# Batch 2's x turned by transfers, two expert units halved, and batch 3's q and k turned half a block sooner

## The chip, the cores and the metric

The kernel runs on one core of a Trainium2 chip. The metric is the device time of one execution in microseconds (us); less is better. The core's engines run side by side, each through its own list of instructions in order, and wait for one another by semaphores: TensorE (PE: matmuls, with weight loads, PEld, beside them), VectorE (DVE), ScalarE (ACT), GpSimd (POOL) and SyncE (SP), which here only issues transfers. A transfer (DMA) is issued by an engine's queue and carried out by the core's 16 DMA engines.

## The reference

Two layers follow each other. The first is attention over 8 batches, 8 heads, 576 positions and head size 64, with a sliding window of 128 and a bias linear in the distance. The second takes its result as 4608 tokens of 512 values through 8 dense experts, whose weights per token come from a table that is normalised by rows and columns in turn, eight times.

```
scores = scale * q @ k.T + bias, masked to 0 <= rel < 128
x      = softmax(scores) @ v                   # reshaped to 4608 x 512
P      = exp(x @ w_gate - max)
8 times: P /= P.sum(1);  P /= P.sum(0);  P *= N / E
out    = sum over e of P[:, e] * (relu(x @ w1[e]) @ w2[e])
```

## The kernel before

**Numbering.** Batches count from 0, so the "third batch" is batch 2 and the "fourth" batch 3. A batch has four blocks of 128 positions and a tail of 64; x block `blk` of batch b is 4b + kb, and the tails of two batches share one of the blocks 32 to 35.

**Stages.** The first stage (to about 250 us) does the attention and, woven between, experts 0 and 1, which don't need the table P. Then the table is normalised, with what is left of experts 0 and 1 filling TensorE. From about 325 us to the end, experts 2 to 7 are done for 18 groups of two blocks in a form of Strassen's product.

**Attention steps.** The loop over `steps` (line 695 on) goes through batch b, key block kb and half of the heads u; `at` = 2 kb + u counts the ten steps of a batch. For the step after, it issues the scores (`psS`, TensorE, line 438), their exponentials (`pt`, ScalarE, line 444) and the mask multiplication (VectorE, line 449). For the step itself it issues the values (`psN`, TensorE, line 472), then on VectorE a reciprocal (line 482) and the normalised x (`xsb`, line 483). The scores of batch b start at the last step of batch b - 1.

**Turning q and k.** q and k are loaded as float32 on SyncE's queue (`load_qk`), cast to `c16` by `cast_qk` (q on VectorE line 298, k on GpSimd line 296 where `pool` is set), and, from batch XPE = 3 on, turned by two transposing transfers on SyncE's queue (`turn_qk`, line 313). `order_qk` (line 324) then copies them into `kN` (GpSimd) and `qN` (VectorE). In batch b, the casts for batch b + 1 stand at steps 8 and 9 of b - 1 and 0 and 1 of b, the transfers and the four `kN` copies at step 1 and the `qN` copies, in pairs, at steps 6 and 7. For batch 3 all four casts stand at steps 0 and 1 of batch 2. Batches 0 to 2 are turned by TensorE.

**Turning x.** Expert matmuls need x with features on partitions (`xT`). `by_pe` says which batches are turned by TensorE: four transposes into `psX` (line 511) and a copy by VectorE (line 522), issued at the next step. The others are turned by one transposing transfer on SyncE's queue per block (line 524). `keep_x` (line 499) also stores each block to DRAM (`xd`) three blocks later, on SyncE's or GpSimd's queue.

**Expert units.** A unit is (expert, first block, number of blocks). Its first layer is eight atoms: four matmuls into `psh` (line 117) and a relu by ScalarE into `hT` (line 129). Its second layer is one atom per block: eight matmuls into `psy` (line 141), then a cast to `yo` by VectorE (line 560) and a store to `ysp` by SyncE (line 546). `hT` has two buffers. `psh`, `psy`, `psN`, `psX` and `psG` (the gates, line 532) share the four banks of the pool tag `pmm` in turn, so each has to wait until the one four places before it has been read.

**Order.** The order is written out at build time, since the program records under a manual schedule. `order` (line 563) lists the units; `Filler` takes the first whose blocks are all below `filler.ready` and deals out its atoms between the attention instructions: per step `filler.fill(1.0)` ahead of the values and the rest of `budget` behind them. `budget` is the backlog of ready units, by the planner's 0.87 us for a first-layer atom of four blocks (`L1_US`) and 1.74 us for a second-layer atom (`L2_US`), divided by the steps left. In batches 0 to 2 `ready` grows block by block; from batch 3 on, at step 0 of each later batch, to all blocks of the batches before.

Of the kernel before, what the change touches and what calls it, by code (L numbers as in the profile page):

```python
# [14 lines left out]
def kernel(  # L15
# [10 lines left out]
    nc = tc.nc  # L26
# [4 lines left out]
    B, H, S, Dh = q.shape  # L31
# [11 lines left out]
    RI = 4  # L43
# [127 lines left out]
    XPE, YO, XSB = 3, 7, 12  # L171
# [61 lines left out]
    if True:  # L233
# [34 lines left out]
        def load_tail(b):  # L268
            t32 = asb.tile([P, H, Dh], FP32, name=f"t32_{b}", tag="s32", bufs=5)
            for lo, src in ((0, q), (TL, k)):  # L270
                nc.sync.dma_start(
                    out=t32[lo : lo + TL], in_=src[b, :, SM:S, :].rearrange("h s d -> s h d")
                )
            tails[b] = t32
# [13 lines left out]
        def cast_qk(b, j, which=(1, 0), pool=False):  # L288

            if b not in c16s:  # L290
                c16s[b] = per.tile([P, 2, RI, H, Dh], FP16, name=f"c16_{b}", tag="a8", bufs=8)
            for n in which:
                src = raw[b][n][:, 2 * j : 2 * j + 2, :].rearrange("p h (i d) -> p i h d", i=RI)
                to = c16s[b][:, n, :, 2 * j : 2 * j + 2, :]
                if pool:
                    nc.gpsimd.tensor_copy(out=to, in_=src)
                elif n == 0:
                    nc.vector.tensor_copy(out=to, in_=src)
                else:
                    nc.scalar.copy(out=to, in_=src)  # L300
# [8 lines left out]
        def turn_qk(b):  # L309
            c16 = c16s.pop(b)  # L310
            qk = per.tile([P, 2, RI, NDT, P], FP16, name=f"qk_{b}", tag="a8", bufs=8)
            for n in range(2):
                nc.sync.dma_start(
                    out=qk[:, n].rearrange("p i j r -> p (i j) r"),
                    in_=c16[:, n].rearrange("p i h d -> p (i h d)"),
                    transpose=True,
                )
            KT[b] = qk
            homes(b)

        def order_qk(b, n, js):

            for j in js:
                (nc.vector, nc.gpsimd)[n].tensor_copy(
                    out=QKT[b][n][:, j].rearrange("p (r i) -> p r i", i=RI),
                    in_=KT[b][:, n, :, j, :].rearrange("p i r -> p r i"),
                )
# [3 lines left out]
        def cast_tail(b):  # L331
            t16s[b] = asb.tile([P, HD], FP16, name=f"t16_{b}", tag="t16", bufs=1)
            nc.gpsimd.tensor_copy(out=t16s[b], in_=tails.pop(b).rearrange("p h d -> p (h d)"))
# [154 lines left out]
            )  # L488

        def by_pe(b):  # L490
            return b < XPE or b == B - 1

        kept: list = []

        def keep_x(left=0):
            while len(kept) > left:
                blk, lo, nk, xsb = kept.pop(0)
                queue = nc.gpsimd if 2 * RI <= blk < 6 * RI else nc.sync
                queue.dma_start(out=xd[blk, lo : lo + nk, :], in_=xsb[0:nk].rearrange("p h d -> p (h d)"))

        def turn_x(b, kb):
            nk = sizes(kb)
            blk = 4 * b + kb if kb < NKB - 1 else 4 * B + b // 2
            lo = 0 if kb < NKB - 1 else TL * (b % 2)
            xT, at = x_of(blk)
            to = xT[:, at, :, lo : lo + nk]
            xsb = xsbs.pop((b, kb))
            if by_pe(b):
                ps = aps.tile([P, NDT, P], FP16, name=f"psX_{b}_{kb}", tag="pmm", bufs=4)
                for j in range(NDT):  # L510
                    nc.tensor.matmul(
                        out=ps[:, j, 0:nk],
                        lhsT=xsb[0:nk, 2 * j : 2 * j + 2, :],
                        rhs=ident[0:nk, 0:nk],
                        is_transpose=True,
                        start=(j == 0),
                        stop=(j == NDT - 1),
                    )
                if b == 0:
                    nc.scalar.copy(out=to, in_=ps[:, :, 0:nk])  # L520
                else:
                    nc.vector.tensor_copy(out=to, in_=ps[:, :, 0:nk])
            else:
                nc.sync.dma_start(out=to, in_=xsb[0:nk].rearrange("p h d -> p (h d)"), transpose=True)
            kept.append((blk, lo, nk, xsb))
            keep_x(3)
# [16 lines left out]
        def store(left=0):  # L543
            while len(stores) > left:
                e, blk, yo = stores.pop(0)
                nc.sync.dma_start(out=ysp[e, blk], in_=yo)
# [15 lines left out]

        order = [(0, 0, 2), (0, 2, 2)]
        for b0 in range(RI, NBLK, 4):
            order += [(0, b0, 4), (1, b0 - 4, 4)]
        order.append((1, NBLK - 4, 4))
        filler = Filler(
            (*unit, lambda unit=unit: unit_atoms(*unit, aps, ("pmm", "pmm"), (4, 4), keep))
# [126 lines left out]
        for n, (b, kb, u) in enumerate(steps):  # L695
            nxt = steps[n + 1] if n + 1 < len(steps) else None
            at = 2 * kb + u
# [44 lines left out]
            if n > 0 and u == 0 and by_pe(steps[n - 1][0]):  # L742
                turn_x(*steps[n - 1][:2])
# [11 lines left out]
            if u == 1 and not by_pe(b):  # L755
                turn_x(b, kb)
# [23 lines left out]
                cast_qk(b + 2, at - 8, (1,), True)  # L780
                cast_qk(b + 2, at - 8, (0,))
            if XPE <= b + 1 < B:
                if at == 0 and b + 1 == XPE:
                    for j in range(2):
                        cast_qk(b + 1, j, (1,), True)
                        cast_qk(b + 1, j, (0,))
                if at < 2:
                    cast_qk(b + 1, at + 2, (1,), True)
                    cast_qk(b + 1, at + 2, (0,))
                if at == 1:  # L790
                    store(1)
                    turn_qk(b + 1)
                    order_qk(b + 1, 1, range(NDT))
                if at == 5:
                    cast_tail(b + 1)
                if at in (6, 7):
                    order_qk(b + 1, 0, range(2 * at - 12, 2 * at - 10))
            if b < B - 1 and at == (1 if b > 1 else 5) and b:
                load_tail(b + 1)
            if 10 * b + at >= 66:  # L800
# [21 lines left out]
        filler.fill(1.0)  # L822
        turn_x(B - 1, NKB - 1)
        keep_x()
        filler.fill(2.6)
        gates(4 * B - 4, NBLK)
# [432 lines left out]
```

## Time and profile before

| | |
|---|---|
| median of 3 runs | 1003.75 us (1002.99 to 1004.34) |
| the profiled execution | 1004.55 us, its span 1002.8 us |
| TensorE busy | 990.0 us, 99% of the span |
| VectorE, ScalarE, GpSimd busy | 762.8, 717.6, 111.0 us |
| batch 2, from its scores to batch 3's | 71.08 to 101.47 us |
| batch 3, from its scores to batch 4's | 101.47 to 133.02 us |
| DMA engines | 122.46 MB, 122 GB/s on average |

A profile row names line, engine, operation and `out<-in`; an `x16` counts instructions, and `idle` or a bracket gives the engine's pause before them and what ended it. A timeline row gives the start and the length of instructions of one kind that follow each other. Matmuls are pipelined, so their lengths overlap; the distance of two starts is the cost. Buffer numbers are left out of names, so `psh` is any first-layer tile; in the text `psh_10_4` is atom 4 of the unit that starts at block 10, and "(b, kb, u)" is an attention step.

### The profile page before, as it was taken

To read this page: it belongs to the slowest core of one execution; us is meant where nothing else is said; L and a number is where in the kernel's file an instruction comes from. 1 tells how busy PE (TensorE), PEld (TensorE's weight loads), DVE (VectorE), ACT (ScalarE), POOL (GpSimd) and SP (SyncE) were. 2 spreads that over 40 slices of the span, in tenths; PEclk is the share of its full clock that TensorE was granted. 3 is DMA by queue.
4 is the path that set the end of the run, shared out by engine and by line. 5 is a ranking of instruction groups with operands and counts; after the bars stand their busy time and mean duration, and the time that the engine had idled before them with its cause. 6 is when DMAs were issued, how large, how long until landed. Compare 5 with 4: busy or idle time off the path is not lost.

```text
span 1002.8 us, 27976 instructions
## 1 busy us (share of the span) xinstructions
PE 990.0 (99%) x11591; PEld 801.7 (80%) x11591; DVE 762.8 (76%) x1598; ACT 717.6 (72%) x1216; POOL 111.0 (11%) x198
## 2 busy tenths in 40 slices
PE   7999999999999999999999999999999999999998
PEld 5655544455544899999999999999999999999997
DVE  6746677666688989887887887787787787787777
ACT  7655554555334768888888888888888888888875
POOL 3314345355010000000000000000000000000000
PEclk9999999999999999999999999999999999999999
DMA  9998799999997324334333333434433333333361
GB/s 244 220 261 212 169 231 227 214 188 172 235 194 167 75 54 97 82 61 99 81 63 93 86 72 79 86 71 79 96 76 64 98 78 66 96 78 67 92 117 48
DMA packets 262895, 122.46 MB, mean 122 GB/s; under 512 B 201968, under 2 KB 253680, under 8 KB 262768
## 3 DMA queue, kind: packets, MB, share of 16 engines
q1 hardware_dynamic: 247264, 100.58, 45.2%
q0 software_dynamic: 15072, 19.93, 11.4%
q8 instruction: 90, 1.47, 0.6%
q14 instruction: 37, 0.30, 0.1%
q10 hardware_dynamic: 432, 0.16, 0.1%
HBM read 78.30 MB, written 23.59 MB: 102 GB/s over the span
## 4 chain that ended last, share of the span: by engine, by line
PE 93%; DVE 3%; DMA 2%; ACT 2%; issue 0%; DVEq 0%; ACTq 0%
PE psM L1030 31%; PE psB L993 14%; PE psh L117 12%; PE psy L141 12%; PE psA L993 9%; PE psC L993 9%; PE psS L438 1%; PE psN L472 1%; DMA k<-in_k_dram 1%; DVE pt L449 1%; ACT pt L444 1%; PE psh L972 1%; DMA xset<-xs 1%; PE psT L368 0%; DVE xsb L483 0%
## 5 line engine op out<-in xcount | busy, mean ns | idle before, releaser
L1030 PEld LDWEIGHTS <-hs 128*128 128x128 f16 x2996 | 271.0, 98 | 22.4 <-DVE hs L1010 0.4
L1030 PE MATMUL psM<-w2l,hs 128*128 128x256 f16 x1440 | 186.6, 273 | 0.2 <-DVE hs L1010 0.2
L993 PEld LDWEIGHTS <-w1l 128*128 128x128 f16 x2848 | 181.4, 98 | 4.8 <-issue 0.2
L1006 ACT ACTIVATE hs<-hs 128x512 f16<-128x512 f16 x212 | 130.3, 629 | 35.7 <-DVE hs L1176 26.1
L1176 DVE TENSOR_TENSOR hs<-psB,s5y 128x512 f16<-128x512 f32 x106 | 73.2, 691 | 98.7 <-ACT xs L902 93.3
L993 PEld LDWEIGHTS <-s 128*128 128x128 f16 x2136 | 141.7, 98 | 7.1 <-issue 0.6
L129 ACT ACTIVATE hT<-psh 128x512 f16<-128x512 f32 (+1 forms) x144 | 84.0, 586 | 76.9 <-PE psh L117 76.9
L117 PE MATMUL psh<-xT,w1t 128*128 128x512 f16 (+1 forms) x608 | 137.5, 368 | 1.1 <-DMA xT<-xsb 1.1
L902 ACT ACTIVATE xs<-xtok,L_sb 128x512 f16<-128x512 f16 x204 | 135.8, 720 | 2.5 <-DMA xset<-xs 2.4
L141 PE MATMUL psy<-w2t,hT 128*128 128x512 f16 x576 | 135.2, 379 | 0.0
L1030 PE MATMUL psM<-more,hs 128*128 128x256 f16 x864 | 129.4, 273 | 0.0
L993 PE MATMUL psB<-xset,s 128*128 128x128 f16 x1424 | 108.5, 219 | 0.5 <-ACT psB L1155 0.5
L993 PE MATMUL psA<-xset,w1l 128*128 128x128 f16 x1424 | 108.5, 219 | 0.0
L444 ACT ACTIVATE pt<-psS 128x1024 f16<-128x1024 f32 x64 | 64.5, 1021 | 58.3 <-PE psS L438 57.4
L141 PEld LDWEIGHTS <-hT 128*128 128x128 f16 x576 | 53.6, 98 | 59.4 <-issue 1.9
L117 PEld LDWEIGHTS <-w1t 128*128 128x128 f16 x608 | 55.2, 98 | 53.8 <-issue 3.9
L1010 DVE TENSOR_TENSOR hs<-hs 128x1024 f16<-128x1024 f16 x107 | 73.8, 690 | 20.4 <-ACT hs L1006 18.3
L1167 ACT COPY psC<-psB 128x512 f32<-128x512 f32 x106 | 60.4, 570 | 38.4 <-PE psB L993 38.4
L449 DVE TENSOR_TENSOR pt<-pt,mask 128x1024 f16<-128x1024 f16 x64 | 52.3, 818 | 38.7 <-ACT pt L444 38.7
L560 DVE CAST yo<-psy 128x512 f16<-128x512 f32 x65 | 44.6, 690 | 44.4 <-PE psy L141 42.0
L1159 ACT COPY s5y<-psC 128x512 f32<-128x512 f32 x106 | 62.2, 587 | 22.4 <-PE psC L993 22.4
L595 POOL DMA_DIRECT2D w2t<-in_moe_w_dram x2 | 1.8, 886 | 668.8 <-DVE xset L926 660.8
(128 smaller groups left out, 1497.2 us busy)
## 6 DMA issues: line engine op xcount, KB each, us to landing
s5y<-ysp SPq DMA_DIRECT2D x36, 256.0 KB, 3.0
ysp<-yo SPq DMA_DIRECT2D x65, 128.0 KB, 4.2
v<-in_v_dram SPq DMA_DIRECT2D x32, 256.0 KB, 5.0
out_dram<-acc SPq DMA_DIRECT2D x31, 256.0 KB, 2.5
q<-in_q_dram SPq DMA_DIRECT2D x5, 1024.0 KB, 7.9
k<-in_k_dram SPq DMA_DIRECT2D x5, 1024.0 KB, 9.0
xtok<-xd SPq DMA_DIRECT2D x34, 128.0 KB, 2.3
w2t<-in_moe_w_dram POOLq DMA_DIRECT2D x4, 1024.0 KB, 12.1
```

Source lines behind the costliest of these rows:

```text
L117: nc.tensor.matmul(out=ps[:, 0:nt], lhsT=w1ts[e][:, dt, P * ft : P * ft + P], rhs=xT[:, at : at + nb, dt, :], start=(dt == 0), stop=(dt == ...
L129: nc.scalar.activation(out=st["hT"][:, ft, 0:nt], in_=ps[:, 0:nt], func=AF.Relu)
L141: nc.tensor.matmul(out=ps, lhsT=st["hT"][:, ft, P * ms : P * ms + P], rhs=w2ts[e][:, ft, :], start=(ft == 0), stop=(ft == NFT - 1),)
L444: nc.scalar.activation(out=pt, in_=ps.rearrange("p a y n -> p (a y) n"), func=AF.Exp, scale=scale)
L449: nc.vector.tensor_tensor(out=pt, in0=pt, in1=mask_of[kb][:, 4 * u : 4 * u + 4, :], op=ALU.mult)
L902: nc.scalar.mul(out=xs[2 * (n % 2) + m], in_=xtok[m], mul=P_sb[:, blk, e : e + 1])
L993: nc.tensor.matmul(out=ps[:, j, :], lhsT=q[k][:, P * j : P * j + P], rhs=xset[n % 2][:, x, P * k : P * k + P], start=(start and j == 0 and ...
L1006: nc.scalar.activation(out=h[n][:, slot], in_=src, func=AF.Relu)
L1010: nc.vector.tensor_tensor(out=t[:, 4:6], in0=t[:, 0:2], in1=t[:, 2:4], op=ALU.add)
L1030: nc.tensor.matmul(out=Ms[bk][:, half, :], lhsT=h[n][:, LEFT[m], f, :], rhs=W2L[e][RIGHT[m]][:, f, :], start=(e == 2 and f == 0 and half = ...
L1159: nc.scalar.copy(out=s5, in_=pc)
L1176: nc.vector.tensor_tensor(out=h[n][:, 3], in0=pb, in1=s5, op=ALU.add)
```

## The change

Three things are changed together.

- `by_pe` leaves out batch 2: its five x blocks are turned by transfers on SyncE's queue, at the second half of their own step. The `xd` stores of batch 1's four full blocks move to GpSimd's queue.
- The units (0,8,4) and (0,12,4) of expert 0 become (0,8,2), (0,10,2) and (0,12,2), (0,14,2). A half unit's first layer has eight atoms of matmuls 256 wide.
- For batch 3, casts 0 and 1 move from step 0 of batch 2 to step 9 of batch 1, casts 2 and 3 to step 0, and `turn_qk` and the `kN` copies from step 1 to step 0.

Because half a unit is ready sooner, expert 0's first half on batch 2 now runs in batch 2's own steps instead of batch 3's. From batch 5 on TensorE's order is the same.

```diff
         def by_pe(b):
-            return b < XPE or b == B - 1
+            return b < XPE - 1 or b == B - 1
...
-                queue = nc.gpsimd if 2 * RI <= blk < 6 * RI else nc.sync
+                queue = nc.gpsimd if RI <= blk < 6 * RI else nc.sync
...
         for b0 in range(RI, NBLK, 4):
-            order += [(0, b0, 4), (1, b0 - 4, 4)]
+            order += [(0, b0, 2), (0, b0 + 2, 2)] if b0 in (4 * XPE - 4, 4 * XPE) else [(0, b0, 4)]
+            order.append((1, b0 - 4, 4))
...
             if XPE <= b + 1 < B:
-                if at == 0 and b + 1 == XPE:
-                    for j in range(2):
-                        cast_qk(b + 1, j, (1,), True)
-                        cast_qk(b + 1, j, (0,))
-                if at < 2:
-                    cast_qk(b + 1, at + 2, (1,), True)
-                    cast_qk(b + 1, at + 2, (0,))
-                if at == 1:
+                first = b + 1 == XPE
+                for j in ((2, 3) if first else (at + 2,)) if at < 2 - first else ():
+                    cast_qk(b + 1, j, (1,), True)
+                    cast_qk(b + 1, j, (0,))
+                if at == 1 - first:
                     store(1)
                     turn_qk(b + 1)
                     order_qk(b + 1, 1, range(NDT))
...
+            if (b, at) == (XPE - 2, 9):
+                for j in range(2):
+                    cast_qk(XPE, j, (1,), True)
+                    cast_qk(XPE, j, (0,))
```

## The prediction

> **What bounds the kernel now.** I read the page's busy times and its chain first, then the timeline of each engine around the batches that the change touches.
>
> ```profile
> PE 990.0 (99%) x11591; PEld 801.7 (80%) x11591; DVE 762.8 (76%) x1598; ACT 717.6 (72%) x1216; POOL 111.0 (11%) x198
> PE 93%; DVE 3%; DMA 2%; ACT 2%; issue 0%; DVEq 0%; ACTq 0%
> L117 PE MATMUL psh<-xT,w1t 128*128 128x512 f16 (+1 forms) x608 | 137.5, 368 | 1.1 <-DMA xT<-xsb 1.1
> ```
>
> TensorE is busy 99% of the span and carries 93% of the chain. From 50 to 325 us it hardly pauses, and after batch 4 both programs give it the same matmuls in the same order. So the time moves by the TensorE work that is removed or added in batches 2 to 4, and by TensorE pauses that go or come there. The only pause that the group lines charge to a transfer in this stage is the 1.1 us for `xT`.
>
> ```profile
> 25.87 3.66 PE L117 MATMUL psh<-xT,w1t 128*128 128x256 f16 x32
> ...
> 95.02 0.41 PE L472 MATMUL psN<-v,pt 128*128 128x65 f16 x8
> 95.26 0.39 PE L511 MATMUL psX<-ident,xsb 128*128 128x128 f16 x4
> 95.48 3.62 PE L141 MATMUL psy<-w2t,hT 128*128 128x512 f16 x16
> ...
> 137.49 0.61 PE L438 MATMUL psS<-qN,kN 64*128 64x256 f16 x8
> 139.22 1.02 PE L117 MATMUL psh<-xT,w1t 128*128 128x512 f16 x4 [1.12 <-DMA xT<-xsb]
> ```
>
> In this TensorE timeline (start, length) the reader is to see the starts: lengths overlap by a drain, so costs are taken from start to start. A turn of x by TensorE (`psX`) costs 0.22 us here (95.26 to 95.48). Matmuls 256 wide come every 0.109 us ((3.66 - 0.27) / 31); those 512 wide every 0.216.
>
> **The change, part by part.** The sum is made against the profiled execution (1004.55 us, span 1002.80) and then taken off the median 1003.75, which is 0.80 lower.
>
> 1. *Batch 2 by transfers.* Twenty transposes leave TensorE: five groups of 0.39 (83.71 to 84.10), 0.22, 0.22, 0.22 and 0.31: -1.36 us. The fourth really spans 0.32, but 0.10 of that is the lead-in of the scores behind it, which stays (132.68 to 133.02 against 95.02 to 95.26); the fifth adds 0.09 to the values ahead of it. VectorE loses four `xT` copies of 0.41 and one of 0.28; it was not what TensorE waited for, so 0. SyncE gains five transposing transfers of 1.25 us issue (median of its 20; 1.20 to 3.21). Queued behind each are the loads of v, t, q and k and the `ysp` stores. Laid out, the second is issued near 90 and lands by 95 (issue to landing 2.3 to 8.9, median 4.3), first used near 100.1; the fourth is issued near 101.3 and used near 109.9. Cost 0; if the slowest landing hits the fourth, 0.3.
>
> 2. *`xd` stores of batch 1 on GpSimd.* Four issues of 0.54 to 0.77 move from SyncE's queue to GpSimd's, between its casts of `c16_3` and of v; the x that they wait for is ready by then. GpSimd stood idle 11.5 us before 91.43, so 0 to TensorE; without that cover, 2.4 us on the casts of v, needed 15 us later. SyncE is freed of four issues, which no one waited for: 0.
>
> 3. *q and k of batch 3 sooner.* Two VectorE casts move ahead of the mask (2,0,1), into an idle stretch of 4.0 us (73.96 to 77.94); the two qk transfers go from 84.32 to about 81.7, ahead of x block (2,0) on SyncE; the four `kN` copies pass the cast of v (3,0). If the load of q lands after 77, the mask is late by the difference, and its values stand at 82.5: 0. `kN` and `qN` of batch 3 were in time before (no gap at 101.47) and are now needed 6 us later: worth 0.
>
> 4. *Units of two blocks.* Sixty-four 512-wide matmuls become 128 of 256: 64 x (0.2184 - 0.216) = +0.15. The stall at 138.03 to 139.22 (1.19 start to start, waiting for the last blocks of batch 3) goes, since unit (0,12,2) needs only blocks 12 and 13: -1.19. Blocks 14 and 15 are needed near 143; their transfers land by 136. A 0.07 wait at 107.7 goes too.
>
> So far -1.36 - 1.19 - 0.07 + 0.15 = -2.47. What is late next comes from two things the order shows. Half units fill the four `pmm` banks twice as fast; and unit (0,8,2) now runs inside batch 2. Batch 3, from its first scores to batch 4's, loses one 1.73 group of `psy` ahead of the unit, half the unit's `psh` (3.4), another `psy` (1.73) and the fifth transpose (0.31): 31.5 becomes 24.3 us, while its work on the other engines stays. Laying the rows end to end in the new order, batch 3's scores start near 107.4 and batch 4's near 131.6 (now 101.47 and 133.02). Four places then come close:
>
> ```profile
> 31.51 0.39 ACT L129 ACTIVATE hT<-psh 128x256 f16<-128x256 f32 x1
> ...
> 106.41 1.02 ACT L444 ACTIVATE pt<-psS 128x1024 f16<-128x1024 f32 x1
> ```
>
> (a) `psh_8_7` takes the bank of the values (2,4,0), which VectorE empties after a `yo` cast and two `qN` copies: ready 105.1, wanted 105.1. 0 to 0.3; I take 0.1.
>
> (b) `psh_10_4` takes the bank of `psh_10_1`, whose relu stands on ScalarE behind the exponentials (3,0,1). Relu of `psh_10_0` at 110.55, exponentials 110.83 to 111.85, relu of `psh_10_1` ends 112.13; wanted 111.77. 0.4 (0 if ScalarE gets to the exponentials later than TensorE to `psh_10_4`, 0.8 with a second relu of 0.38 ahead).
>
> (c) `psh_12_5` takes the bank of the values (4,0,1), emptied behind the mask (4,1,0): wanted 138.96, ready 139.0 with a mask of 0.69, 139.8 with one of 1.46. 0.05 to 0.85; I take 0.4.
>
> (d) The second half of batch 4's scores, wanted near 131.9, needs the last two `qN` copies. VectorE's row there is mask (3,3,1) from 127.5, reciprocal and x 0.55, two `qN`, a `yo` cast 0.61, reciprocal and x 0.55, two `qN`.
>
> ```profile
> 126.99 1.29 DVE L449 TENSOR_TENSOR pt<-pt,mask 128x1024 f16<-128x1024 f16 x1 [0.66 <-ACT pt L444]
> 128.20 0.17 DVE L482 RECIPROCAL rden<-psN 128x4 f32<-128x4 f32 x1
> ...
> 139.22 1.46 DVE L449 TENSOR_TENSOR pt<-pt,mask 128x1024 f16<-128x1024 f16 x1
> ...
> 225.22 2.39 DVE L324 COPY qN<-qk 128x512 f16<-128x512 f16 x2
> ...
> 123.15 4.58 POOL L324 COPY kN<-qk 128x512 f16<-128x512 f16 x4 [11.12 <-DMA qk<-c]
> ```
>
> These VectorE and GpSimd rows show why the prices have two ends: a mask is 0.69 alone (117.48) and 1.29 or 1.46 beside GpSimd copies; two `qN` are 1.10 alone, 2.39 beside GpSimd. Undisturbed, the last `qN` ends at 132.0, a stall of 0.1; with 1.29, 2.39 and 1.52 (the pair at 228.07), 134.2, a stall of 2.3. The `kN` copies now fall on that very stretch (rival 1), so I take the middle, 1.2. The Trainium skill (SBUF — State Buffer, "Who interferes with whom") says that VectorE instructions with two SBUF inputs, and copies in two-port modes, share a port pair with GpSimd as an exclusive lock. The rows above agree; by that rule the upper end of (d) would apply whenever both engines copy at once.
>
> Sum: -2.47 + 0.1 + 0.4 + 0.4 + 1.2 = -0.37 us: 1004.2 as profiled, 1003.4 against the median. ScalarE's sixteen more relus (32 x 0.38 against 16 x 0.60, +2.6 us) lie in its idle time except at (b).
>
> **The rivals.**
> 1. *Slower: k of batch 4 comes late in the short batch 3.* From the values (b,0,1) to the last `kN` copy took 17.3 us in batch 3 (110.47 to 127.73), and 19.0, 18.9 and 18.3 in batches 4 to 6; the new order leaves 18.0. Besides, the load of v (4,0), now queued on SyncE behind the fifth x transfer near 112.6 (it was issued at 103.31), stands on GpSimd ahead of the last cast of k: beyond some 7 us to landing (3.9 median, 8.9 worst in the x stage) it delays everything behind it, by up to 2.2. Worst 1.0 + 2.2 = 3.2 in place of (d)'s 1.2, and with (b) and (c) at 0.4 and 0.85: +2.1, 1005.8. It beats the gain from a stall of 1.6 at (d) on. For it: the margin of 18.0 against 17.3 to 19.0; against it: the median landings hide it.
> 2. *Faster: the new waits are hidden.* (a) to (d) at their low ends, 0 + 0.4 + 0.05 + 0.1: -1.9, 1001.8; without (b), 1001.4. For it: TensorE starts in this stage show no wait for a bank above 0.15 us. Against it: those units are twice as wide.
> 3. *Narrow matmuls cost more.* If weight loads don't hide behind narrow matmuls, a half costs its load: at 0.142 (the longest load row, the float32 turns), 64 x (0.284 - 0.216) = 4.4 us in place of 0.15, and the time is 1007.6. Against it: starts 0.109 apart at 256 columns. The Trainium skill (TensorE: Matmul & The Clock Gate, "Back-to-back issue gap") speaks for it: sustained gaps of 81 ns at 128 columns and 131 at 512. By that rule, with an estimated 98 ns at 256 on a line between them, the change adds 64 x 0.065 = 4.2 us and the sum is +3.7; the rows agree with neither rate (0.216 at 512), and they decide.
> 4. *The stall is not removed*: the gate of batch 4 (`psG`) then waits for `xT` instead. It stands 8 us later: +1.2, 1004.6.
>
> **How the numbers follow.** Forecast 1003.4, chance 0.52 (its own range 1002.3 to 1004.6, from (c) and (d)); rival 1 0.20, rival 2 0.24, rivals 3 and 4 0.02 each. Low end: rival 2 without (b), 1001.4; high end: rival 1 short of its worst, 1005.4. Runs of this kernel spread 0.13%, so 0.2% (2.0 us) is about what a measurement can tell from no change. Faster by that needs all four stalls under 0.5 together: two thirds of rival 2, and 0.02 of the forecast, 0.18. Slower needs 4.5 of stalls: half of rival 1, rival 3 and 0.02 of the forecast, 0.14. The rest, 0.68, is within.
>
> **What would show it.** Right: no `psX` of batch 2; no wait for `xT` near 137; batch 4's scores start near 132 to 134; short TensorE gaps near 112, 132 and 139, released by ScalarE and VectorE; `kN` copies beside `qN` copies. Wrong: a TensorE gap over 2 us near 132 (rival 1), none (rival 2), 256-wide starts above 0.109 apart (rival 3), or a gap anywhere outside 100 to 145 us.

## The result and the profile after

The change is slower. Its median is 1008.49 us (13 runs, 1006.55 to 1011.77) against 1004.87 us for the kernel before beside it (13 runs): a ratio of 1.0035, 95% interval [1.0023, 1.0047]. The forecast was 1003.4 us, with a range of 1001.4 to 1005.4 and a chance of 0.14 for slower. A second set of runs of the same change gave 1.0033 [1.0019, 1.0047]. The profiled execution took 1007.75 us with a span of 1006.0 us, 3.2 more than before.

From the page of the change: busy times, the chain's shares, and the row of the first expert layer.

```profile
PE 989.3 (98%) x11635; PEld 806.6 (80%) x11635; DVE 767.1 (76%) x1593; ACT 719.2 (71%) x1232; POOL 111.4 (11%) x202
PE 89%; DVE 5%; DMA 3%; ACT 2%; issue 1%; SPq 1%; POOL 0%; DVEq 0%; ACTq 0%
L117 PE MATMUL psh<-xT,w1t 128*128 128x512 f16 (+1 forms) x672 | 138.7, 349 | 1.1 <-DVE xsb L483 0.5
```

TensorE has 0.7 us less to do and takes 3.2 longer. Its part of the chain went from 93 to 89%: the lost time is waits, and `xT` is no longer what the first layer waits for most. The TensorE timeline of the change (start, length) around batch 4's first scores, whose eight matmuls now come in three pieces, and where batch 3's x is used:

```profile
132.17 0.39 PE L438 MATMUL psS<-qN,kN 64*128 64x256 f16 x4
134.30 0.28 PE L438 MATMUL psS<-qN,kN 64*128 64x256 f16 x2 [1.74 <-DVE qN L324]
135.22 0.29 PE L438 MATMUL psS<-qN,kN 64*128 64x256 f16 x2 [0.64 <-DVE qN L324]
135.44 1.90 PE L141 MATMUL psy<-w2t,hT 128*128 128x512 f16 x8
...
143.34 1.05 PE L117 MATMUL psh<-xT,w1t 128*128 128x256 f16 x8 [0.50 <-DVE xsb L483]
```

Counted from start to start, that is place (d) of the prediction with 2.74 us instead of 1.2, and (c) with 0.67 instead of 0.4. The brackets name VectorE's copies of q. This is VectorE's timeline of the change, then GpSimd's:

```profile
129.07 2.81 DVE L324 COPY qN<-qk 128x512 f16<-128x512 f16 x2
...
132.95 2.23 DVE L324 COPY qN<-qk 128x512 f16<-128x512 f16 x2
```

```profile
128.94 4.86 POOL L324 COPY kN<-qk 128x512 f16<-128x512 f16 x4 [10.16 <-DMA qk<-c]
...
133.79 0.94 POOL L404 CAST v<-v 128x512 f16<-128x512 f32 x1
```

The first pair of `qN` lies wholly on GpSimd's four `kN` copies (128.94 to 133.80), the second on the last of them and then on the cast of v behind it. Before, GpSimd was done with `kN` at 127.73, 5.3 us ahead of the scores, and the pairs took:

```profile
128.74 1.11 DVE L324 COPY qN<-qk 128x512 f16<-128x512 f16 x2
...
131.76 1.10 DVE L324 COPY qN<-qk 128x512 f16<-128x512 f16 x2
```

The two pairs together are 2.83 us longer, about the 2.74 of the stall. But VectorE was not alone late: the last of the scores also need the last `kN` copy, done at 133.80, and undisturbed they would have started near 132.5. With the `qN` copies in time, up to 1.3 of the 2.74 would have stayed (an estimate from these rows). Measured from batch 3's first scores the `kN` copies start where they did (128.94 - 107.37 = 21.6 us, before 123.15 - 101.47 = 21.7). It is TensorE's batch 3 that got shorter under them: 24.8 us instead of 31.55.

With -2.47 for what was removed, and 0.09, 0.45, 0.67 and 2.74 for (a) to (d), the stretch should be 1.48 us longer; from batch 2's first scores to the point from which TensorE's order is the same (169.6 before) it is 1.55. Two more losses come after the place where I had looked. Near 207 us a mask that runs beside GpSimd casts takes 1.92 us instead of 0.69 and costs 0.9; in the second set's profile this did not come, but 0.86 for `xT` near 173 did. And near 367 us, from the TensorE timeline of the change, then VectorE's:

```profile
367.98 0.60 PE L1032 MATMUL psM<-w2f,hs 128*128 128x256 f16 x4 [0.40 <-DVE w2f L636]
...
372.64 0.61 PE L995 MATMUL psB<-xset,w1l 128*128 128x128 f16 x8 [0.54 <-DVE hs L1178]
```

```profile
365.91 1.42 DVE L1052 SCALAR_TENSOR_TENSOR acc<-s5y,L_sb,acc 128x512 f32<-128x512 f16 x2 [1.75 <-DMA s5y<-ysp]
```

Before, VectorE waited 0.56 us for this load. Start to start the two gaps are 0.56 and 0.59 longer than before: 1.15 us, some 200 us behind the point from which TensorE's order is the same.

### The profile page after: what moved, and what is told of

It is laid out like the page before. It is cut to its first block, busy times and chain, and to the rows that moved or that the text cites. A ratio compares the mean times of both kernels' runs of the same rounds, so it can differ in the third digit from the quotient of the medians.

```text
span 1006.0 us, 28094 instructions
## 1 busy us (share of the span) xinstructions
PE 989.3 (98%) x11635; PEld 806.6 (80%) x11635; DVE 767.1 (76%) x1593; ACT 719.2 (71%) x1232; POOL 111.4 (11%) x202
## 3 DMA queue, kind: packets, MB, share of 16 engines
q8 instruction: 91, 1.49, 0.6%
## 4 chain that ended last, share of the span: by engine, by line
PE 89%; DVE 5%; DMA 3%; ACT 2%; issue 1%; SPq 1%; POOL 0%; DVEq 0%; ACTq 0%
PE psM L1032 31%; PE psB L995 14%; PE psh L117 12%; PE psy L141 11%; PE psA L995 9%; PE psC L995 9%; PE psN L472 1%; PE psS L438 1%; DMA v<-in_v_dram 1%; DMA xset<-xs 1%; DVE pt L449 1%; DVE qN L324 1%; ACT pt L444 0%; DMA s5y<-ysp 0%; PE psT L368 0%
## 5 line engine op out<-in xcount | busy, mean ns | idle before, releaser
L129 ACT ACTIVATE hT<-psh 128x512 f16<-128x512 f32 (+1 forms) x160 | 86.2, 545 | 84.5 <-PE psh L117 83.8
L117 PEld LDWEIGHTS <-w1t 128*128 128x128 f16 x672 | 61.1, 98 | 50.3 <-issue 3.4
L1161 ACT COPY s5y<-psC 128x512 f32<-128x512 f32 x106 | 62.1, 586 | 21.6 <-PE psC L995 21.6
```

Source lines behind the costliest of these rows:

```text
L117: nc.tensor.matmul(out=ps[:, 0:nt], lhsT=w1ts[e][:, dt, P * ft : P * ft + P], rhs=xT[:, at : at + nb, dt, :], start=(dt == 0), stop=(dt == ...
L129: nc.scalar.activation(out=st["hT"][:, ft, 0:nt], in_=ps[:, 0:nt], func=AF.Relu)
L1161: nc.scalar.copy(out=s5, in_=pc)
```

## The experiments

Batches count from 0 here; the expectations on record say "third batch" for batch 2, "fifth" for batch 4, and stand in each section in the order of the experiments' numbers. "Unit 8" is (0,8,4), "unit 12" (0,12,4). "Shift" is how much later the last attention scores come than before, counted from batch 2's first scores (which start at 69.8 to 74.2 us, as the start-up differs); like the wait, it is read from one profile of each. In 4 and 9 the wait includes a stretch at half clock, told of under experiments 4 and 5; in 8 that stands behind the plus sign. The last column counts the runs whose mean granted TensorE clock was 0.998 or less.

| kernel | ratio to before, 95% | shift, us | wait at batch 4's scores, us | clock low |
|---|---|---|---|---|
| change | 1.0035 [1.0023, 1.0047] | 2.46 | 2.74 | 10 of 13 |
| change again | 1.0033 [1.0019, 1.0047] | 2.80 | 2.4 | 6 of 12 |
| 1: only unit 12 halved | 1.0031 [1.0018, 1.0044] | 1.21 | 0 | 8 of 12 |
| 2: only unit 8 halved | 1.0021 [1.0008, 1.0035] | 2.12 | 2.7 | 6 of 12 |
| 3: none halved | 1.0033 [1.0019, 1.0047] | 2.23 | 0 | 3 of 8 |
| 4: before, unit 8 halved | 1.0045 [1.0030, 1.0060] | 5.68 | 5.2 | 5 of 6 |
| 5: before, unit 12 halved | 0.9993 [0.9980, 1.0007] | 0.45 | 0 | 2 of 12 |
| 6: q, k of batch 4 sooner | 1.0029 [1.0011, 1.0046] | 4.06 | 0 | 4 of 12 |
| 7: `kN` of batch 4 on ScalarE | 1.0030 [1.0014, 1.0047] | 3.01 | 1.0 | 4 of 12 |
| 8: code moved | 1.0026 [1.0010, 1.0041] | 3.64 | 2.3 + 1.7 | 7 of 10 |
| 9: x of batch 2 on TensorE | 1.0068 [1.0051, 1.0085] | 5.88 | 4.9 | 5 of 6 |
| 10: 7 and unit 16 halved | 1.0028 [1.0012, 1.0043] | 4.04 | 1.0 | 0 of 10 |
| 11: q, k of batch 3 back | 1.0042 [1.0027, 1.0057] | 1.94 | 2.8 | 7 of 9 |
| 12: 1, last block on TensorE | 1.0014 [1.0001, 1.0026] | 1.27 | 1.4 | 2 of 12 |
| 13: 3, last block on TensorE | 1.0034 [1.0018, 1.0050] | 4.92 | 1.3 | 3 of 12 |

The kernel before, in the four sets of runs in which its clock was noted beside these: 15 of 109.

### 1 to 3: which half makes the waits

Three edits of one line; the last line in each fence is the experiment's. First 1, then 2, then 3, which halves none:

```diff
-            order += [(0, b0, 2), (0, b0 + 2, 2)] if b0 in (4 * XPE - 4, 4 * XPE) else [(0, b0, 4)]
+            order += [(0, b0, 2), (0, b0 + 2, 2)] if b0 == 4 * XPE else [(0, b0, 4)]
```

```diff
+            order += [(0, b0, 2), (0, b0 + 2, 2)] if b0 == 4 * XPE - 4 else [(0, b0, 4)]
```

```diff
+            order += [(0, b0, 2), (0, b0 + 2, 2)] if b0 < 0 else [(0, b0, 4)]
```

> The change with unit (0,8,4) whole again; only (0,12,4) is halved. Batch 3 is as long as before. Theory 1 (the shortened batch 3 makes kN late and puts it beside qN): the scores of batch 4 wait for no qN or kN (under 0.3 us against 2.7 in the change), the bank wait near 112 goes, the one near 143 stays (0.4 to 0.8), the wait for xT near 137 stays away. Start of batch 7's first scores against before: -1.4 - 1.2 + 0.2 + 0.6 = -1.8 us; time 0.1 to 0.3% under before. Theory 2 (the transfers of x and the moved xd stores are what costs): the scores of batch 4 still wait 2 us or more; time 0.2 to 0.4% above before.

> The change with unit (0,12,4) whole again; only (0,8,4) is halved. Theory 1: batch 4's scores wait 2 to 3 us for qN and kN as in the change, the bank wait near 112 (0.4) is there and the one near 143 is not; the whole unit (0,12,4) may wait for xT again, less than 1.2 us, since the scores' own wait has given the transfers time. Start of batch 7's first scores against before: +1 to +2.5 us. Theory 2: the same wait. A theory 3, that halved units as such cost by their banks: no more than 0.5 us at batch 4's scores.

> The change with no unit halved: x of batch 2 by transfers, the xd stores of batch 1 on GpSimd and q and k of batch 3 sooner, alone. Theory 1: no wait at batch 4's scores; the wait for xT near 137 is back, 1.2 to 2 us; start of batch 7's first scores against before: -1.4 + 0 to 0.8 = -1.4 to -0.6 us; time 0 to 0.15% under before. Theory 2: batch 4's scores or the values wait 2 us or more; time 0.2% or more above before.

TensorE's timeline of experiment 1, then of experiment 2:

```profile
105.42 2.75 PE L117 MATMUL psh<-xT,w1t 128*128 128x512 f16 x12 [3.33 <-DMA xT<-xsb]
```

```profile
133.96 0.29 PE L438 MATMUL psS<-qN,kN 64*128 64x256 f16 x2 [1.74 <-DVE qN L324]
134.88 0.28 PE L438 MATMUL psS<-qN,kN 64*128 64x256 f16 x2 [0.64 <-DVE qN L324]
```

Of the two halves it is unit 8's that brings the wait at batch 4's scores: experiment 2 has it to the hundredth, 1 and 3 do not. But 1 and 3 were not foreseen either: a whole unit 8 needs batch 2's last block, whose transfer is issued at 101.85, behind a transfer of 4.51 us and two stores of 2.88 on SyncE's queue, and TensorE stands 3.3 us for it (3.30 in experiment 3). So the transfers of batch 2 do not cost 0: with the halved unit their lateness is covered, and the cover costs the other wait. Experiment 1's ratio is larger than its shift of 1.2 us; its clock was low in 8 of 12 runs (next section). Its four other runs, in the median, are still 2.0 us above the runs of the kernel before whose clock was not low, so the clock is not all of it; the rest is open.

### 4 and 5: the halves alone, on the kernel before

Experiment 4 is this; in 5 the condition is `b0 == 4 * XPE`:

```diff
-            order += [(0, b0, 4), (1, b0 - 4, 4)]
+            order += [(0, b0, 2), (0, b0 + 2, 2)] if b0 == 4 * XPE - 4 else [(0, b0, 4)]
+            order.append((1, b0 - 4, 4))
```

> The kernel before with only unit (0,8,4) halved; x of batch 2 is turned by TensorE, q and k of batch 3 as before. Batch 3 is shortened as in the change. Theory 1: batch 4's scores wait 1.5 to 3 us for qN and kN, so that the start of batch 7's first scores is 1 to 3 us later than before, time 0.1 to 0.3% above. Theory 2: without the added transfers no such wait (under 0.5 us), time within 0.1% of before.

> The kernel before with only unit (0,12,4) halved. The wait for xT near 138 (1.2 us) goes; by theory 1 a bank wait of 0.4 to 0.8 us comes some 6 us later, and batch 4's scores don't wait. Start of batch 7's first scores against before: -0.3 to -0.8 us; time within 0.2% of before. If the stall only moves to the gates or to the second half unit, -0.1 to +0.3 us.

TensorE's timeline of experiment 4, then of experiment 5:

```profile
136.07 0.28 PE L438 MATMUL psS<-qN,kN 64*128 64x256 f16 x2 [1.69 <-DVE qN L324]
137.85 0.40 PE L438 MATMUL psS<-qN,kN 64*128 64x256 f16 x2 [1.50 <-DVE qN L324]
```

```profile
144.49 1.05 PE L117 MATMUL psh<-xT,w1t 128*128 128x256 f16 x8 [0.31 <-DVE xsb L483]
```

Halving unit 8 brings the wait without any transfer of batch 2's x: it is the short batch 3 that does it. Halving unit 12 does what the prediction said: the 1.19 at 138 is gone and 0.31 for a bank comes at (c); batch 7's first scores come 0.46 us sooner. (The 0.45 of the table is later: a wait of 0.83 for `xT` comes behind them, at 241.23.) It is the only edit of this study that is not slower, and its gain is too small to be told from none.

Experiment 4 lost more than its two waits, and more than the 1 to 3 us on record, and so showed a cost that I had not thought of. From its windows (busy time of PE, PEld, DVE, ACT and POOL with their instructions, then the granted clock, DMA share, GB/s):

```profile
134.44:137.85 3.41, 0.29 (x3) 0.10 (x2) 3.38 (x6) 1.00 (x1) 2.96 (x8) 1.00 1.07 365
137.85:141.26 3.41, 3.41 (x10) 1.27 (x10) 1.98 (x5) 1.02 (x1) 0.00 (x0) 0.50 1.19 255
```

After a window of 3.41 us with 0.29 us of matmuls, the clock was 0.50 for the next 3.41 us: 512-wide matmuls came 427 ns apart instead of 216, and 1.7 us were lost. Experiments 8 (136.17 to 139.59) and 9 (138.89 to 142.31) show the same behind the same wait. Within a profile such stretches start whole multiples of 3.413 us apart (34 such lengths lie between 22.84 and 138.89 in experiment 9), so they mark out windows of this length. The change's own two profiles have none at this wait, but a stretch of 3.41 us at half speed takes 0.0017 off the mean clock, and 16 of the change's 25 runs had 0.998 or less, against 15 of 109 before. Over the table: with 2.3 us or more at batch 4's scores it is 46 of 68 runs, with 1.4 or less there and no wait over 2.5 us elsewhere (5, 6, 7, 10, 12) 12 of 58; 1, 3 and 13, with a wait of 2.6 to 3.3 elsewhere, have 14 of 32. (These bounds were set after the runs.) So each run stakes 1.7 us on a wait of that size. For the runs that were not profiled this is inferred from their mean clock; where in them the clock fell is not recorded. It need not be at this wait: the profiles of 5, 6, 9 and 13 have such a stretch in the start-up, at 25.97, 17.48, 22.84 and 9.01 us, where the edits change nothing, and in 5 and 6 it is what makes the mean low.

### 6, 7 and 10: take the wait at the scores away

Experiment 6 casts batch 4's q and k in steps 8 and 9 of batch 2, and turns and copies them at step 0 of batch 3:

```diff
-                cast_qk(b + 2, at - 8, (1,), True)
-                cast_qk(b + 2, at - 8, (0,))
+                for j in (2 * at - 16, 2 * at - 15) if b + 1 == XPE else (at - 8,):
+                    cast_qk(b + 2, j, (1,), True)
+                    cast_qk(b + 2, j, (0,))
...
-                first = b + 1 == XPE
-                for j in ((2, 3) if first else (at + 2,)) if at < 2 - first else ():
+                first = b < XPE + 1
+                for j in ((2, 3) if b + 1 == XPE else () if first else (at + 2,)) if at < 2 - first else ():
```

Experiment 7 leaves the times and gives batch 4's `kN` copies to ScalarE, in pairs at steps 6 and 7 of batch 3:

```diff
-                (nc.vector, nc.gpsimd)[n].tensor_copy(
+                (nc.scalar.copy if act else (nc.vector, nc.gpsimd)[n].tensor_copy)(
...
-                    order_qk(b + 1, 1, range(NDT))
+                    if b != XPE:
+                        order_qk(b + 1, 1, range(NDT))
...
+                    if b == XPE:
+                        order_qk(b + 1, 1, range(2 * at - 12, 2 * at - 10), True)
```

Experiment 10 adds to it that the unit on batch 4, (0,16,4), is halved:

```diff
-            order += [(0, b0, 2), (0, b0 + 2, 2)] if b0 in (4 * XPE - 4, 4 * XPE) else [(0, b0, 4)]
+            order += [(0, b0, 2), (0, b0 + 2, 2)] if b0 in (4 * XPE - 4, 4 * XPE, 4 * XPE + 4) else [(0, b0, 4)]
```

> The change with batch 4's q and k also half a block sooner: casts 0 and 1 at step 8 and casts 2 and 3 at step 9 of batch 2, transfers and kN copies at step 0 of batch 3 instead of step 1. Theory 1a (kN and qN stand beside each other because the transfers land late in a short batch 3): kN copies end before 130 instead of 133.7, the wait at batch 4's scores falls from 2.7 to 0 to 1.3 us, start of batch 7's first scores against before +0.2 to -1.2 us. If the wait stays above 2 us, lateness isn't its cause.

> The change with batch 4's kN copies on ScalarE, in pairs at steps 6 and 7 of batch 3, instead of on GpSimd at step 1; the transfers stay late. Theory 1b (VectorE's qN copies are slowed by GpSimd's kN copies): the two pairs of qN copies take 1.1 us each instead of 2.8 and 2.2, and the wait at batch 4's scores falls under 0.8 us. Theory 1a alone (the late landing of q and k is what counts, the slowing is nothing): the pairs stay above 2 us, or the wait stays above 1.5 us.

> The change with the fifth batch's kN copies on ScalarE (as in the run before with that edit) and expert 0's unit on the fifth batch halved as well. Theory 1 (what the shorter wait at the scores gained was given back because the whole unit on the fifth batch waits for the last of its four x transfers, 2.4 us at 174.8 us): that wait falls to at most 0.3 us and is not replaced, the shift from the third batch's start to the eighth's work falls from 3.0 to 0.5 to 1.0 us; 64 more matmuls take TensorE's code packet half a period away from the load of s5y, which lands in 2.9 to 3.0 us, and the ratio to before is 0.999 to 1.001. Theory 2 (SyncE's queue and the VectorE copies are co-bound there, so that a wait moves only): a new wait of 1.5 us or more near 170 to 215 us, shift 2 us or more, ratio 1.002 to 1.003.

GpSimd's timeline of experiment 6, then VectorE's and TensorE's:

```profile
126.50 4.58 POOL L324 COPY kN<-qk 128x512 f16<-128x512 f16 x4 [10.11 <-DMA qk<-c]
```

```profile
132.70 1.11 DVE L324 COPY qN<-qk 128x512 f16<-128x512 f16 x2
```

```profile
135.66 0.65 PE L438 MATMUL psS<-qN,kN 64*128 64x256 f16 x8
```

With the `kN` copies done at 131.08, ahead of both `qN` pairs, the pairs take 1.11 and 1.10 and batch 4's scores come in one piece. So the lateness of q and k in the short batch 3 is a cause of the wait, as the theory on record had it. Its forecast of the shift, +0.2 to -1.2 us, failed with 4.06: other waits came instead, 0.46 and 0.84 near 140.6 and 143.2, 1.77 for `xT` at 177.5 and 1.1 near 212.

VectorE's timeline of experiment 7, with `kN` off GpSimd, then its TensorE:

```profile
128.87 1.11 DVE L324 COPY qN<-qk 128x512 f16<-128x512 f16 x2
...
131.04 1.22 DVE L324 COPY qN<-qk 128x512 f16<-128x512 f16 x2
```

```profile
133.28 0.28 PE L438 MATMUL psS<-qN,kN 64*128 64x256 f16 x2 [0.69 <-ACT kN L324]
...
174.81 1.02 PE L117 MATMUL psh<-xT,w1t 128*128 128x512 f16 x4 [2.36 <-DMA xT<-xsb]
```

The pairs are back at 1.11 and 1.22, at almost the same point: it was GpSimd's copies that stretched them. The wait shrank to 1.0 (under 0.8 was expected), now for ScalarE's `kN`, and nothing was won: 2.36 us for batch 4's last x transfer came at 174.8. Experiment 10 halves the unit that waits there. The wait for `xT` is gone, and this comes instead, on TensorE, then VectorE:

```profile
175.42 0.29 PE L472 MATMUL psN<-v,pt 128*128 128x65 f16 x4 [1.53 <-DVE yo L560]
```

```profile
174.67 0.69 DVE L560 CAST yo<-psy 128x512 f16<-128x512 f32 x1 [1.71 <-DMA ysp<-yo]
```

VectorE can't write `yo` until an older one is stored, and the stores stand on SyncE's queue between the transposing transfers, which take 1.2 to 1.8 us to issue there (a store behind one 2.97). The second theory's forecast on record came true (a new wait of 1.5 us or more, a shift of 2 or more). That SyncE's queue is close to being the bound there itself, so that a TensorE that comes sooner meets it at the next tile, is how I read these rows; no run freed the queue. The clock was low in 0 of 10 runs against 4 of 12 in experiment 7, which can be chance.

### 9, 12 and 13: what the transfers are worth

Experiment 9 takes the transfers back:

```diff
-            return b < XPE - 1 or b == B - 1
+            return b < XPE or b == B - 1
...
-                queue = nc.gpsimd if RI <= blk < 6 * RI else nc.sync
+                queue = nc.gpsimd if 2 * RI <= blk < 6 * RI else nc.sync
```

Experiments 12 and 13 are 1 and 3 with batch 2's last whole block turned by TensorE, the other four by transfers:

```diff
-        def by_pe(b):
-            return b < XPE - 1 or b == B - 1
+        def by_pe(b, kb):
+            return b < XPE - 1 or b == B - 1 or (b == XPE - 1 and kb == NKB - 2)
```

> The change with x of the third batch turned on TensorE again (both halved units, q and k of the fourth batch sooner). Theory 1 (what the transfers save on TensorE, 1.36 us, is saved in full where the units are halved, and the waits before the fifth batch's scores come from the halved third-batch unit alone): waits before those scores of 1.5 to 5 us as in the change and in the kernel before with that unit halved (5.2), shift from the third batch's start to the eighth's work 3 to 5 us, ratio to before 1.004 to 1.006. Theory 2 (SyncE's queue, on which the transfers lie, is what makes later loads late, and so takes the saving back): the wait for v and for q and k shrinks, ratio 1.000 to 1.003. For the load of s5y near 362 us: 20 more transposes on TensorE bring its code packets 1.8 us earlier, to about 0.8 us ahead of the issue; by the code packet theory it lands in 2.9 to 3.5 us.

> The change with only the fourth batch's unit halved and the last whole block of the third batch turned on TensorE; its other three blocks and its tail go by transfers. Theory 1 (the transfers save what they take off TensorE, and only the late landing of the last one cost the 3.3 us in the run with that unit halved): the 3.3 us near 105 us fall to at most 0.5; four of the five groups of transposes stay away (4/5 of 1.36 = 1.1 us), the wait of 1.19 us near 138 us stays away, no wait comes before the fifth batch's scores; the shift from the third batch's start to the eighth's work is -1.0 to -2.0 us, the ratio to before 0.998 to 0.9995, and few runs show a granted clock of 0.998. Theory 2 (the other transfers of that batch land late as well, as they share SyncE's queue with q, k and v): a wait of 1 to 3 us near 102 to 107 us stays, ratio 1.000 to 1.003.

> The same with no unit halved. Theory 1: as above near 105 us, but the wait for xT near 138 us comes back (1.1 to 1.3 us); shift from the third batch's start to the eighth's work -0.5 to +0.2 us, ratio 0.999 to 1.0005. Theory 2: a wait of 1 to 3 us near 102 to 107 us and the one near 138 us, ratio 1.0015 to 1.004.

Under halved units the transfers are worth having: without them the kernel loses another 0.33% (3.3 us), since 1.36 us of transposes return and the wait at the scores grows to 4.9 us, the clock's share in it (a shift of 3 to 5 us was expected, 5.88 came). Under whole units they aren't. TensorE of experiment 12, then VectorE, GpSimd:

```profile
103.52 2.76 PE L117 MATMUL psh<-xT,w1t 128*128 128x512 f16 x12 [0.50 <-DMA xT<-xsb]
...
133.80 0.29 PE L438 MATMUL psS<-qN,kN 64*128 64x256 f16 x2 [1.19 <-DVE qN L324]
...
172.30 1.02 PE L117 MATMUL psh<-xT,w1t 128*128 128x512 f16 x4 [0.82 <-DMA xT<-xsb]
```

```profile
131.04 2.71 DVE L324 COPY qN<-qk 128x512 f16<-128x512 f16 x2
```

```profile
125.55 5.36 POOL L324 COPY kN<-qk 128x512 f16<-128x512 f16 x4 [13.71 <-DMA qk<-c]
...
130.91 0.61 POOL L404 CAST v<-v 128x512 f16<-128x512 f32 x1
```

The 3.3 us wait fell to 0.5, as the first theory said, but the rest of its forecast (0.998 to 0.9995) failed: with batch 3 at its old length (32.1 us), the `kN` copies now start 25.6 us after its first scores instead of 21.7. The first `qN` pair meets them (2.34 us); the second, shown above, comes behind their end at 130.91 and meets the casts of v and t that follow them on GpSimd up to 133.3. And `xT` is late again at 172. Experiment 13 waits 1.34 near 107, 1.3 at the scores and 2.62 for `xT` at 145, then at half clock. Against experiment 5 (0.9993), four transfers, the moved stores and q and k of batch 3 sooner (which by experiment 11 moves nothing) make 1.0014; the two intervals overlap. Which transfer of the queue delays `qk` by those 4 us I did not settle.

### 8 and 11: the late load near 362 us, and q and k of batch 3

Experiment 8 puts 40 transposes of 64 rows ahead of batch 1's own, which overwrite their results:

```diff
+                for j in range(2 * NDT) if b == 1 else ():
+                    nc.tensor.matmul(
+                        out=ps[:, j % NDT, 0:TL],
+                        lhsT=xsb[0:TL, 2 * (j % NDT) : 2 * (j % NDT) + 2, :],
+                        rhs=ident[0:TL, 0:TL],
+                        is_transpose=True,
+                        start=True,
+                        stop=True,
+                    )
```

Experiment 11 puts batch 3's casts, transfers and `kN` copies back to where the kernel before has them:

```diff
-                first = b + 1 == XPE
-                for j in ((2, 3) if first else (at + 2,)) if at < 2 - first else ():
-                    cast_qk(b + 1, j, (1,), True)
-                    cast_qk(b + 1, j, (0,))
-                if at == 1 - first:
+                if at == 0 and b + 1 == XPE:
+                    for j in range(2):
+                        cast_qk(b + 1, j, (1,), True)
+                        cast_qk(b + 1, j, (0,))
+                if at < 2:
+                    cast_qk(b + 1, at + 2, (1,), True)
+                    cast_qk(b + 1, at + 2, (0,))
+                if at == 1:
...
-            if (b, at) == (XPE - 2, 9):
-                for j in range(2):
-                    cast_qk(XPE, j, (1,), True)
-                    cast_qk(XPE, j, (0,))
```

> The change with 40 additional 64-row transposes (their results are overwritten by the same values) in the second batch, which only move TensorE's instruction stream: by 131 matmuls per 11.9 us between two code packets near 360 us, 40 more matmuls before it bring each packet about 3.6 us earlier against the work. Theory 1 (the load of s5y near 362 us lands 1.1 us late because a 16 KB code packet of 1.0 to 1.45 us starts 0.7 to 1.1 us after the load is issued): the packet now starts about 2.6 us before the load, the load lands in 2.9 to 3.0 us instead of 4.0, VectorE waits 0.6 to 0.8 for it instead of 1.75, and the two gaps on TensorE near 367 and 372 (0.40 and 0.54 by the page's releasers, together 1.0 to 1.4) go. Theory 2 (the late load belongs to the order that the halved units bring): 4.0, and both gaps stay. In total the additional matmuls cost 1.2 to 2.4 us in the second batch, so theory 1 gives the change plus 0.2 to 1.4 us, theory 2 the change plus 1.2 to 2.4 us.

> The change with q and k of the fourth batch cast and turned where the kernel before does it (steps 0 and 1 of the third batch). Theory 1 (the sooner cast is free, and as expert 0's first half runs within the third batch, the fourth batch's scores start 5 to 6 us later than before, so that q and k would be in time unmoved): the same as the change within 0.1%, no wait before the fourth batch's scores, x transfers of the third batch issued in front of q and k. Theory 2 (the move is needed): a wait of 1 us or more before the fourth batch's scores, which start that much later, ratio 1.0045 or more. The load of s5y near 362 us keeps landing in about 4.0 us, as TensorE's instruction count is the same.

About every 129 matmuls (of which each brings a weight load; 90 packets on 11591 in the kernel before) the trace has one packet of 16 KB on a queue of the kind "instruction", 0.9 to 2.2 us long; by that distance I take it for TensorE's code. In the change one starts 1.03 us after the issue of the `s5y` load, at 362.9. The transfers of the change from 361.8 to 366.2 us, then of the kernel before from 359.4 to 363.8 (issues: size, us from issue to landing):

```profile
q8 instruction: 1, 0.02, 2.1%
...
s5y<-ysp SPq DMA_DIRECT2D x1, 256.0 KB, 4.0
```

```profile
s5y<-ysp SPq DMA_DIRECT2D x1, 256.0 KB, 2.9
```

In the profiles in which the packet starts 0.7 to 1.1 us after the issue (the change, twice, 6, 7 and 11) the load is used 3.8 to 4.2 us after it; in the others (packet at least 1.4 us ahead, or 2.3 us or more behind) 2.9 to 3.0. In experiment 9 the packet, 1.45 us ahead of the load, meets the `xset` transfer issued before it: that lands in 3.99 us instead of 2.4, and 0.7 us of the gaps is there though the load is in time. Experiment 8 adds only instructions, in batch 1, and moves the packet to 3.14 us ahead. Its VectorE, with the wait of before:

```profile
366.25 1.42 DVE L1061 SCALAR_TENSOR_TENSOR acc<-s5y,L_sb,acc 128x512 f32<-128x512 f16 x2 [0.68 <-DMA s5y<-ysp]
```

Of the 1.15 us of gaps 0.07 are left. The total can't tell (1.0026; the interval holds the change's 1.0035): the added matmuls make batch 2's start 1.4 us later, counted from batch 1's first scores, and the profiled run had its clock halved (2.3 us of waits at the scores, then 1.7). Experiment 11 keeps the number of TensorE's instructions and keeps the loss: there the packet hits the `xset` transfer ahead of the load, VectorE waits 1.85 us for it, and the gaps are 0.98. Its interval holds the change's 1.0035, and no wait comes at batch 3's scores: turning q and k of batch 3 sooner neither helped nor hurt. (Undone, it leaves a new wait of 0.5 us for a bank near 101, and a shift that is 0.5 us less.)

### The change again

> The changed kernel once more, for a second profile and a second interval. Theory 1: the waits at batch 4's scores (2.7 us), near 112 (0.45) and near 143 (0.7) come again at the same places and sizes within 0.2 us, since the order fixes them. The 0.9 us near 207 and the 0.9 us near 370 of the first profile, which no theory explains yet, either come again (then the change causes them) or not (then they differ from run to run). Time 0.2 to 0.5% above before.

The stall at the scores came again (0.96 and 1.11 by the brackets, 2.4 start to start), and so did the bank waits and the 1.1 us near 367. The 0.9 near 207 did not; 0.86 for `xT` came at 173.85 in its place. In this set the runs at a clock of 0.999 or more have a median of 1006.9 (6 runs), those of the kernel before 1004.22 (31): +2.7 us, as much as the 1.55 of the first profile's local stretch and the 1.15 of the late load. The rest of the measured +3.3 has about the size of the clock's part: low in 0.64 of the change's runs against 0.14 before, 0.5 x 1.7 = 0.85. But both profiles of the change have one more wait of 0.9 us, near 207 or near 173, which this sum leaves out, so the shares are an estimate. Why these waits come in one run and not in the next is open; experiment 5 has one too (0.83 at 241).

## Why the prediction was wrong

**Steps 1 and 4, the sum of -2.47: right.** `psX` of batch 2 is gone, so is the 1.19 for `xT`; 256-wide matmuls come 109 ns apart, so rival 3 fell, as did rival 4. But "cost 0" in step 1 holds only while unit 8 is halved (experiments 1, 3); I had priced two steps apart that hang on each other.

**Step 2** (stores on GpSimd) was only undone together with the transfers, in experiment 9; by itself it wasn't tried. **Step 3** cost 0, as said (experiment 11).

**(a), (b), (c): right,** 0.09, 0.45 and 0.67 for 0.1, 0.4 and 0.4.

**(d): this step failed.** I took the middle, 1.2, between copies undisturbed (0.1) and disturbed (2.3). It measured 2.74, past the upper end, in which the pairs had 2.39 and 1.52 us; GpSimd's `kN` copies and the cast of v behind them lay beside both, and they took 2.81 and 2.23. I had written that the `kN` copies "now fall on that very stretch" and still halved the price: with two engines certain to copy at once, the disturbed row is the price, not one end of it. And (d) priced the `qN` copies alone, while the last `kN` copy was late as well (rival 1). The rule quoted from the Trainium skill (SBUF — State Buffer, "Who interferes with whom") gave the upper end for that case, and the trace agrees: with `kN` on ScalarE the same pairs take 1.11 and 1.22.

**Rival 1** named the right place, the `kN` copies, and much of the way: at 116.76 GpSimd had waited 3.47 us for the load of v (4,0), ahead of the last cast of k. From the values (3,0,1) at 114.18 to the last `kN` copy at 133.80 it is 19.6 us where the new order left 18.0, so k was 1.6 us late, and with it up to 1.3 of the 2.74 would have stayed whatever VectorE did. Counted from batch 3's first scores the copies start no later than before (21.6 us against 21.7): it is the batch that became short. What (d) had beyond that came through VectorE's `qN`. Rival 1's worst case, +2.1, is near the 1.55 of the local stretch.

**What was in no term:** 1.15 us of a load delayed by a packet of 16 KB, and some 0.85 us of halved clock. With them: 1.55 + 1.15 + 0.85 = 3.55, measured 3.3 (the second set) and 3.6 (the first). The clock's part is an estimate over runs, the other two stand in the profile. The local 1.55 alone, on the 1003.75 of the prediction, gives 1005.3, just inside the range, where the measured ratio gives 1007.3; it is these terms that led out of it. The range had no room for them, because every term of it lay between 100 and 145 us; the prediction named a gap outside as what would show it wrong, and gave it no price.

## What to carry to other kernels

When work is moved out of a stage, price what still has to be done under its shorter length: the copies of batch 3 stayed where they were and its matmuls left. A new wait of the bounding engine can cost more than its length, here 1.7 us more, once it empties most of one window of its clock. And where a queue runs near full beside the bounding engine, a wait that is taken away comes back at the next tile, so test a pair of edits as a pair: here the transfers gained only with unit 8 halved, and no kernel with unit 8 halved was as fast as the one before.

## What the runs showed of the hardware

- **The clock drops on a window that is not idle.** The Trainium skill (TensorE: Matmul & The Clock Gate, "Part 1: The HAM clock gate") says that the array goes to half rate after an idle window of about 3.4 us that runs freely. The length agrees (3.41 us at 0.50, in three profiles behind this wait), and so does the free run: the windows lie differently over the same wait from profile to profile. But the windows ahead of it had 0.29, 0.85 and 1.49 us of matmuls in them (experiments 4, 9, 8), and in the start-up 0.91, 1.12, 1.40 and 1.69 (13, 5, 9, 6). One of 1.49 in experiment 1, of 1.64 in 3 and 6 and of 1.68 in the change were let pass (placed by the half-clock stretch at the end of each span). So a window need not be idle here; between 1.49 and 1.69 us of 3.41 both happened.
- **Packets that I take for code get in the way of loads.** One of 16 KB, 1.45 us long, made a 256 KB load land in 4.0 us instead of 2.9; 40 more matmuls some 300 us earlier moved it away.
- **Copies on GpSimd and VectorE slow each other, VectorE's the more:** a pair of VectorE's 512-wide copies takes 1.1 us alone and 2.2 to 2.8 beside GpSimd's copies and casts; a `kN` copy of GpSimd's takes 1.06 alone (experiment 6) and up to 1.5 beside `qN` (the change).
